# Attention and MLP in parallel on one core: full-size products in four column groups, value steps of two key tiles, VectorE's share of the exponentials set by set

## Chip, core and metric

The kernel runs on one core of a Trainium2 chip. The metric is the device time of the core in microseconds (us). It is a single launch, with all inputs read from and the output written to device memory.

## What is computed

From a 2048 x 512 input the reference takes a layer norm, gives it to an attention of 32 heads (16 wide each) and to an MLP with a second layer norm, and adds both results to the input:

```python
x = A_x                                   # 1 x 2048 x 512, bf16
xn = _layernorm(x, axis=-1)
# attention: H = 32 heads, Dh = 16, scale = 16 ** -0.5
qkv = (xn @ wqkv).reshape(B, S, 3, H, Dh)
scores = einsum("bhqd,bhkd->bhqk", q, k) * scale
o = einsum("bhqk,bhkd->bhqd", softmax(scores), v)
a = o.reshape(B, S, D) @ wo
# MLP: F = 1792
h = gelu(_layernorm(xn) @ w1 + b1)        # tanh form
return x + a + h @ w2 + b2
```

## The kernel before

**Sets.** The work of the attention is cut into 32 sets g: four blocks of 512 queries (qt = g // 8) times eight groups of four heads (s = g % 8). A set goes over 16 key tiles of 128 keys. One key tile of one head is a unit: a 128 x 512 piece of scores. `qk` (L918, its product at L921) makes a unit's scores on TensorE: the four heads of a set lie in four 32-row groups of the array, so up to four units run side by side. A unit then takes one of two ways.

**ScalarE's way.** `build_tile` (L1018) takes three units (PSUM banks 0 to 2) or two (banks 3 and 4) in turn, makes their scores, and ScalarE (ACT) takes the exponential of all of them in one instruction (L1046) into `p_sb`, a ring of 15 units. While it works on one group of banks, TensorE fills the other.

**VectorE's way.** For the key tiles that `KD_OF` names (2, 5, 8 and 11 in each set from set 2 on), the scores "ride" with a tile of ScalarE's into bank 5 or 7 (`ride`, `rides`). VectorE (DVE) turns them into 16-bit numbers with an add and a maximum (L1085, one instruction for each unit), and makes four shifted copies of the four units (L1108, four instructions for each key tile). Read as fp16 bits, these five terms with five sets of weighted values approximate the exponential; `dve_terms` (L1095) issues the value products of the terms in steps of two, two and one.

**Value products.** `pv` (L930, product at L939) multiplies the values with the exponentials. The values of four heads lie in four groups of 32 columns of the array, so four products run side by side, all into bank 6 (the accumulator of a set, closed by the copy at L1141). ScalarE's key tiles have one such group of four each, issued by `build_pv` (L1055) tile by tile; VectorE's have five.

**Full-size products.** Everything else on TensorE uses 128 x 128 weights: the transposes (L679), the projections to keys and queries (L746) and to values (L818), the MLP's first matrix (L1242), its second matrix and the output projection (`chain`, L1264, product at L1272, four products to a step), the last output products (L1337), and the filler products that keep TensorE busy (L1390).

**What sets the order.** Nothing is issued as it is written. Each piece of work goes as an `_Op` with a duration, a priority (mostly a due time) and resources into a planner, `_Plan` (L61). Its `run` (L124) goes through a modelled time and gives each engine, among the ops that could start within `TOL` of the earliest, the one with the lowest priority number. TensorE's ops have a mode: "q" for scores, "p" for value products, "d" for full-size products. A change of mode is charged 0.11 us, and an op of the same mode as the last gets its priority lowered by `KEEP`. The order that comes out is fixed in the program; on the chip each engine goes through its own list and waits where an input is late.

**Once per query block** come the MLP (14 first-matrix blocks, evicted by VectorE at L1249, two GELU instructions on ScalarE at L1259, then the second matrix) and the output projection. A set's sums of exponentials go through device memory to be inverted and spread (L1143 to L1153), and GpSimd checks their range (L1162 to L1168). The last set does this on VectorE (`build_opost_last`, L1172). After the plan has run, two small products and a cast (L1402 to L1405) make a flag of the range; a branch on it would recompute everything in a safe way (`_general`), which these inputs do not need.

Of the kernel before, what the change touches and what calls it, by code (L numbers as in the profile page):

```python
# [22 lines left out]
P = 128  # L23
DH = 16
HS = 4
# [26 lines left out]
class _Op:  # L52

    __slots__ = ("eng", "dur", "fn", "ndeps", "outs", "prio", "acq", "rel", "lat", "ready", "end",
                 "done", "dense", "mode", "seq", "spare")
# [5 lines left out]
class _Plan:  # L61
# [9 lines left out]
    TOL = 0.25  # L71
    KEEP = 0.5
# [51 lines left out]
    def run(self):  # L124
# [7 lines left out]
        while left:  # L132
# [41 lines left out]
            op.end = end  # L174
# [261 lines left out]
def kernel(  # L436
# [30 lines left out]
    KD = (2, 5, 8, 11)  # L467
    KD_OF = [() if g < 2 else KD for g in range(NG)]
# [22 lines left out]
    b2_sb = const.tile([1, D], BF, name="b2_sb")  # L491
# [26 lines left out]
    NQB = 5  # L518
# [16 lines left out]
    ta = const.tile([P, QW], F32, name="ta")  # L535
    rl_t = const.tile([P, NCH], F32, name="rl_t")
    on_t = const.tile([P, NCH, 32], BF, name="on_t")
    okl = const.tile([P, 2, NCH], F32, name="okl")
    okrow = flagp.tile([P, 1], F32, name="okrow")
    okr = flagp.tile([P, 1], F32, name="okr")  # L540
# [8 lines left out]
    add = I.add  # L549

# [94 lines left out]
    def layernorm(g):  # L645
        tt = range(4 * g, 4 * g + 4)
        sl = slice(4 * g, 4 * g + 4)
        after = [xt_op[2], xt_op[3]] if g else []
        for t in tt:
            def fst(t=t):  # L650
                I(nc.vector.bn_stats(out=stats[:, t, :], in_=x_sb[:, t, :]))  # L651
                st_inst[0] = I(nc.vector.bn_aggr(out=mv[:, t, :], in_=stats[:, t, :]))
            st_op[t] = add("DVE", 0.77, fst, [ld_x[t]] + after,
                           T0 + KG * g - 8 + t % 4 * 0.2 if g else -50 + t, lat=0.1)
        pr = T0 + KG * g - 7.5 if g else -40

        def frs():
            I(nc.gpsimd.tensor_scalar(out=wv1[:, sl], in0=mv[:, sl, 1], scalar1=LN_EPS,
                                      scalar2=None, op0=ALU.add))
            I(nc.gpsimd.tensor_tensor(out=r1[:, sl], in0=wv1[:, sl], in1=mhalf[:, sl],  # L660
                                      op=ALU.pow))
        r = add("POOL", 0.9, frs, [st_op[t] for t in tt] + [mk_half], pr)
        pool = early if g else wide
        for t in tt:
            r1_op[t] = r
            pr = T0 + KG * g - 7 + t % 4 * 0.2 if g else -30 + t
            eng = "DVE"

            def fxn(t=t):
                I(nc.vector.tensor_scalar(  # L670
                    out=xn_r[:, t % 4, :], in0=x_sb[:, t, :], scalar1=mv[:, t, 0:1],
                    scalar2=r1[:, t:t + 1], op0=ALU.subtract, op1=ALU.mult))
            xo = add(eng, 0.33, fxn, (r, xn_op.get(t - 4)), pr)
            key = ("xt", t)

            def ftr(t=t, key=key):
                bk = pool.bank(key)
                for jc in range(JC):
                    I(nc.tensor.matmul(ps[:, bk, jc * P:(jc + 1) * P],  # L679
                                       lhsT=xn_r[:, t % 4, jc * P:(jc + 1) * P], rhs=ident_bf[:],  # L680
                                       start=True, stop=True))
# [36 lines left out]
    ld_b2 = dma("SP", b2_sb[:], B_b2[None, :], (ld_w2,), prio=62.0, lat=4.0)  # L718
# [23 lines left out]
    def project(pool, key, pr, nb, deps, w, b, qt, slow=False):  # L742
        def fmm():
            bk = pool.bank(key)
            for jc in range(JC):
                I(nc.tensor.matmul(ps[:, bk, :], lhsT=w[:, jc, b * P:(b + 1) * P],  # L746
                                   rhs=xnT[:, qt, jc, :], start=(jc == 0), stop=(jc == JC - 1)))
# [66 lines left out]
    def vmm(pool, key, t):  # L814
        def fn():
            bk = pool.bank(key)
            for jc in range(JC):
                I(nc.tensor.matmul(ps[:, bk, :],  # L818
                                   lhsT=xnT[:, t // TQ, jc, (t % TQ) * P:(t % TQ + 1) * P],
                                   rhs=wv_sb[:, jc, :], start=(jc == 0), stop=(jc == JC - 1)))  # L820
        return fn
# [196 lines left out]
    def build_tile(i):  # L1018
# [10 lines left out]
        deps = set()  # L1029
        for (g, k, j) in us:  # L1030
            need_q(g)
            deps.update(qk_deps(g, k))
        acq = [(res[b0 + x], ("t", i)) for x in range(n)] + [(ride(i), None)]
        q = add("PE", pen(1), fqk, list(deps) + [qk_prev[0]], dl - QO, acq=acq, mode="q")
# [14 lines left out]
        e = add("ACT", act(n * QW), fex, [q, exp_prev[0]] + list(set(free)), dl,  # L1049
# [5 lines left out]
    def build_pv(u0):  # L1055
        g, k, _ = units[u0]

        def fpv():
            pv(g, k, [(va[:, k, :], lambda j: p_sb[:, unit_slot[u0 + j], :])])
        o = add("PE", pen(1), fpv, set([unit_exp[u0 + j] for j in range(HS)]  # L1060
                                       + [va_op[k], va_op[min(k + 1, NT - 1)]]),
                due(u0 + 4) - PO, acq=((o_ready, g),), mode="p")
        for j in range(HS):
            pv_of_unit[u0 + j] = o
# [107 lines left out]
    def build_opost_last(g):  # L1172
# [3 lines left out]
                 pv_ops[g], pr, rel=(o_ready,))  # L1176
# [11 lines left out]
        def f2():  # L1188
            I(nc.vector.tensor_scalar(out=okl[:, 0, :], in0=tav[:, :, DH], scalar1=L_MIN,
                                      scalar2=None, op0=ALU.is_ge))  # L1190
            I(nc.vector.tensor_scalar(out=okl[:, 1, :], in0=tav[:, :, DH], scalar1=L_MAX,
                                      scalar2=None, op0=ALU.is_le))
            I(nc.vector.tensor_tensor(out=okl[:, 0, :], in0=okl[:, 0, :], in1=okl[:, 1, :],
                                      op=ALU.mult))
            I(nc.vector.tensor_reduce(out=okr[:], in_=okl[:, 0, :], op=ALU.min, axis=AX.X))
        add("DVE", 0.6, f2, [e1], pr + 30)
# [10 lines left out]
    def build_mlp(qt):  # L1207
# [10 lines left out]
        def ft():  # L1218
            for i in range(4):
                I(nc.tensor.matmul(ps[:, misc.bank(rkey), i * P:(i + 1) * P], lhsT=rt[:, i, :],  # L1220
                                   rhs=ident_bf[:], start=True, stop=True))
# [11 lines left out]
        for fc in range(FC):  # L1233
# [6 lines left out]
            def fh(n=n, key=key):  # L1240
                for jc in range(JC):
                    I(nc.tensor.matmul(ps[:, misc.bank(key), :], lhsT=w1_r[:, n % NW1, jc, :],  # L1242
                                       rhs=yT[:, jc, :], start=(jc == 0), stop=(jc == JC - 1)))
# [20 lines left out]
    def chain(key, pr, steps, deps):  # L1264

        m = None
        for f0 in range(0, len(steps), 4):
            part = steps[f0:f0 + 4]

            def fn(part=part, f0=f0):  # L1270
                for y, (a, b) in enumerate(part):
                    I(nc.tensor.matmul(ps[:, misc.bank(key), :], lhsT=a, rhs=b,  # L1272
                                       start=(f0 + y == 0), stop=(f0 + y == len(steps) - 1)))
# [6 lines left out]
    def build_down(qt, gl):  # L1280

        del h_use[:]
        for c in range(TQ):
# [8 lines left out]
            steps += [(ones_bf[0:1, 0:P], b2_sb[0:1, :])]  # L1292
# [34 lines left out]
    def build_final():  # L1327
        gs = (NG - 2, NG - 1)
        for c in range(TQ):
# [5 lines left out]
            def fm(g, key=key, cs=cs):  # L1335
                def fn():
                    I(nc.tensor.matmul(ps[:, tailp.bank(key), :], lhsT=ont[:, g % NON, cs],  # L1337
                                       rhs=wo_pad[:, (g % NS) // 2, g % 2, :], start=(g == gs[0]),
                                       stop=(g == gs[1])))
# [11 lines left out]
    for g in range(NG):  # L1351
# [4 lines left out]
        while ti < len(tiles) and tiles[ti][2] < stop:  # L1356
            build_tile(ti)
            end = tiles[ti][2] + tiles[ti][1]
            while pend + HS <= end:
                build_pv(pend)  # L1360
                pend += HS
# [15 lines left out]
    def fill(t0, t1):  # L1377
        got = []
        t = max(t0, 2.5)
        while t + 0.25 < t1:  # L1380
# [20 lines left out]

    nc.vector.tensor_reduce(out=okrow[:], in_=okall[:], op=ALU.min, axis=AX.X)  # L1402
    nc.tensor.matmul(ps[0:1, OB, 0:1], lhsT=okrow[:], rhs=onesp[:], start=True, stop=False)
    nc.tensor.matmul(ps[0:1, OB, 0:1], lhsT=okr[:], rhs=onesp[:], start=False, stop=True)
    nc.vector.tensor_copy(flag_i[:], ps[0:1, OB, 0:1])  # L1405
    fast_ctx.close()
    full = 2 * P
# [33 lines left out]
```

## Time and profile before

| | us |
|---|---|
| median of 3 runs | 878.18 (876.96 to 879.3) |
| the profiled execution | 877.14 |
| its span, first to last instruction | 875.3 |

| engine | busy us | share of the span |
|---|---|---|
| PE (TensorE products) | 789.1 | 90% |
| DVE (VectorE) | 780.0 | 89% |
| ACT (ScalarE) | 771.8 | 88% |
| POOL (GpSimd) | 55.7 | 6% |

The profile shows one execution. PEld is TensorE's loading of weights, which overlaps its products. A row of a group gives a line of the kernel, the engine, the output and inputs, the tile's size, the count, the busy time and mean duration of one, and the idle time of the engine just before, with what ended it. Consecutive instructions overlap a little in the records, so a mean duration is longer than the distance from one start to the next.

### The profile page before, as it was taken

What the parts mean: (1) busy time and instruction counts of PE and PEld (TensorE: products, weight loads), DVE (VectorE), ACT (ScalarE), POOL (GpSimd) and SP (SyncE); (2) the same over time, 40 slices, a digit from 0 to 9 for tenths busy, and PEclk for the clock granted to TensorE, in tenths of its full rate; (3) what the DMA queues carried; (4) which work ended last, traced back from release to release, by engine and by line L of the source; (5) the groups of instructions that cost most, each with busy time, mean ns of one, the idle gap of its engine ahead of it and who ended that gap; (6) DMA issues with size and microseconds to landing.
All of it is one profiled execution on the core that took longest, in us unless ns stands there. A gap on an engine that the chain in (4) does not pass through costs nothing.

```text
span 875.3 us, 17469 instructions
## 1 busy us (share of the span) xinstructions
PE 789.1 (90%) x7007; PEld 248.6 (28%) x7007; DVE 780.0 (89%) x1346; ACT 771.8 (88%) x667; POOL 55.7 (6%) x153
## 2 busy tenths in 40 slices
PE   8999999889988999899888999999978999989895
PEld 3332232222222322223222322223222322223221
DVE  8645999988899999968989999987899999988986
ACT  4798888989899888999999888999999979899883
POOL 2300000000000000000000000000000000000000
PEclk9999799999999999999989999989999999999998
DMA  5400111000001112000001111000001111100000
GB/s 169 109 1 2 38 51 50 13 21 21 20 9 26 39 43 51 20 19 10 13 14 32 33 44 51 16 17 21 21 15 26 33 44 32 38 19 21 20 15 28
DMA packets 54810, 27.65 MB, mean 32 GB/s; under 512 B 40645, under 2 KB 50630, under 8 KB 54722
## 3 DMA queue, kind: packets, MB, share of 16 engines
q1 hardware_dynamic: 52562, 24.76, 10.3%
q10 hardware_dynamic: 2160, 1.70, 0.7%
q8 instruction: 56, 0.92, 0.4%
q14 instruction: 32, 0.26, 0.1%
HBM read 23.85 MB, written 2.61 MB: 30 GB/s over the span
## 4 chain that ended last, share of the span: by engine, by line
DVE 53%; PE 25%; ACT 10%; issue 8%; DMA 3%; POOL 0%; SPq 0%; DVEq 0%; ACTq 0%
DVE x_sb L1085 20%; DVE tb_x L1108 13%; ACT p_sb L1046 10%; PE ps L939 8%; PE ps L921 7%; DVE x_sb L1108 6%; PE ps L1272 5%; DVE ht L1249 4%; DMA rlb<-rdram 2%; DVE ont L1155 1%; DVE osb L1141 1%; PE ps L746 1%; PE ps L818 1%; PE ps L1390 1%; DVE stats L651 1%
## 5 line engine op out<-in xcount | busy, mean ns | idle before, releaser
L1046 ACT ACTIVATE p_sb<-ps 128x1024 bf16<-128x1024 f32 (+1 forms) x640 | 731.2, 1232 | 76.8 <-PE ps L921 69.8
L1085 DVE TENSOR_SCALAR x_sb<-ps 128x512 int16<-128x512 f32 x480 | 324.2, 689 | 32.7 <-PE ps L921 31.8
L921 PE MATMUL ps<-qz,kt 32*128 32x512 bf16 x2048 | 285.5, 389 | 43.2 <-ACT p_sb L1046 30.6
L1108 DVE TENSOR_SCALAR tb_x<-x_sb 128x2048 int16<-128x2048 int16 x320 | 217.7, 690 | 4.9 <-PE ps L939 3.4
L939 PE MATMUL ps<-p_sb,va 128*32 128x512 bf16 x1568 | 153.4, 394 | 4.5 <-DVE osb L1141 4.4
L921 PEld LDWEIGHTS <-kt 32*128 32x128 bf16 x2048 | 76.1, 91 | 247.9 <-issue 240.7
L939 PE MATMUL ps<-tb_x,vs 128*32 128x512 f16 x1280 | 121.2, 391 | 9.5 <-DVE tb_x L1108 8.4
L1108 DVE TENSOR_SCALAR x_sb<-x_sb 128x2048 int16<-128x2048 int16 x160 | 110.4, 690 | 1.9 <-PE ps L939 1.1
L939 PEld LDWEIGHTS <-va 128*32 128x32 bf16 x2048 | 50.7, 95 | 117.2 <-issue 108.1
L939 PEld LDWEIGHTS <-vs 128*32 128x32 bf16 x1920 | 56.0, 95 | 96.1 <-issue 82.4
L939 PE MATMUL ps<-x_sb,vs 128*32 128x512 f16 x640 | 64.5, 391 | 5.6 <-DVE x_sb L1108 5.0
L1162 POOL TENSOR_SCALAR okt<-lc 128x16 f32<-128x16 f32 x31 | 17.0, 548 | 761.0 <-DMA lc<-ldram 761.0
L1242 PE MATMUL ps<-yT,w_r 128*128 128x512 bf16 x224 | 57.7, 380 | 5.5 <-DVE x_sb L1085 3.6
L1272 PE MATMUL ps<-w_sb,ht 128*128 128x512 bf16 x224 | 59.5, 383 | 0.0
L939 PE MATMUL ps<-x_sb,va 128*32 128x512 f16 x480 | 48.9, 397 | 0.5 <-DVE osb L1141 0.5
L1249 DVE TENSOR_SCALAR ht<-ps,b_sb 128x512 bf16<-128x512 f32 x56 | 42.1, 752 | 0.0
L1390 PE MATMUL ps<-ones_bf,zeros_bf 128*128 128x512 bf16 x90 | 33.9, 455 | 1.5 <-DVE ones_bf L613 1.5
L1272 PE MATMUL ps<-wo_pad,ont 128*128 128x512 bf16 x120 | 32.0, 387 | 0.2 <-DVE x_sb L1085 0.2
L1242 PEld LDWEIGHTS <-w_r 128*128 128x128 bf16 x224 | 19.2, 97 | 37.6 <-issue 23.6
L1155 DVE TENSOR_TENSOR ont<-osb,rlb 128x512 bf16<-128x512 f32 x31 | 21.4, 690 | 7.0 <-DMA rlb<-rdram 7.0
L1272 PEld LDWEIGHTS <-ht 128*128 128x128 bf16 x224 | 18.1, 98 | 30.5 <-issue 17.5
L1259 ACT ACTIVATE ht<-ht 128x3584 bf16<-128x3584 bf16 x8 | 25.1, 3182 | 0.0
(89 smaller groups left out, 339.7 us busy)
## 6 DMA issues: line engine op xcount, KB each, us to landing
rlb<-rdram SPq DMA_DIRECT2D x31, 256.0 KB
w_r<-in_B_w_dram SPq DMA_DIRECT2D x56, 128.0 KB
x_r<-in_A_x_dram SPq DMA_DIRECT2D x16, 128.0 KB
w_sb<-in_B_w_dram SPq DMA_DIRECT2D x1, 1792.0 KB
out_dram<-ot SPq DMA_DIRECT2D x12, 128.0 KB
x_sb<-in_A_x_dram SPq DMA_DIRECT2D x2, 512.0 KB
wkv<-in_A_wqkv_dram ACTq DMA_DIRECT2D x1, 512.0 KB
x_sb<-in_A_x_dram ACTq DMA_DIRECT2D x1, 512.0 KB
```

Of the source, the lines that this page charges most:

```text
L921: I(nc.tensor.matmul(ps[:, bank, :], lhsT=kt[lo:lo + 32, s // 2, k * P:(k + 1) * P], rhs=qz[lo:lo + 32, (qt * NB + s // 2) % NQB, s % 2, : ...
L939: I(nc.tensor.matmul(ps[32 * j:32 * j + 32, o_bank[g], :], lhsT=vals[:, h * VS:h * VS + 32], rhs=wts(j), start=st, stop=(pv_left[g] == 0), ...
L1046: I(nc.scalar.activation(p_sb[:, s0:s1, :].rearrange("p a b -> p (a b)"), ps[:, b0:b0 + n, :].rearrange("p a b -> p (a b)"), AF.Exp, scale ...
L1085: I(nc.vector.tensor_scalar(out=ib[sl][:, j, :], in0=ps[:, misc.bank(key), :], scalar1=LEVEL, scalar2=0.0, op0=ALU.add, op1=ALU.max))
L1108: I(nc.vector.tensor_scalar(out=tb[x % NTB].rearrange("p j q -> p (j q)"), in0=ib[sl].rearrange("p j q -> p (j q)"), scalar1=float(SHIFT[t ...
L1155: e4 = add("DVE", dve(QW), lambda: I(nc.vector.tensor_tensor(out=ont[:, slot, :], in0=osb[:, i2, :], in1=rlb[:], op=ALU.mult)), [e3] + lis ...
L1162: I(nc.gpsimd.tensor_scalar(out=okt[:, 0, :], in0=lc[:, i2, :], scalar1=L_MIN, scalar2=None, op0=ALU.is_ge))
L1242: I(nc.tensor.matmul(ps[:, misc.bank(key), :], lhsT=w1_r[:, n % NW1, jc, :], rhs=yT[:, jc, :], start=(jc == 0), stop=(jc == JC - 1)))
L1249: I(nc.vector.tensor_scalar(out=ht[:, fc, :], in0=ps[:, misc.bank(key), :], scalar1=b1_sb[:, fc:fc + 1], scalar2=None, op0=ALU.add))
L1259: I(nc.scalar.activation(out=hv, in_=hv, func=AF.Gelu_apprx_tanh, scale=1.0))
L1272: I(nc.tensor.matmul(ps[:, misc.bank(key), :], lhsT=a, rhs=b, start=(f0 + y == 0), stop=(f0 + y == len(steps) - 1)))
L1390: I(nc.tensor.matmul(ps[:, OB if opened is None else o_bank[opened], :], lhsT=zeros_bf[:], rhs=ones_bf[:], start=opened is None, stop=open ...
```

## The change

All 896 full-size products are written as four products of 32 columns each, one to each column group of the array, as the value products are (`mm`, L552 of the changed kernel); the filler products too. They get the planner's mode "p", so that only two modes are left. The one-row product with the bias b2 becomes one of 128 rows (b2 padded with zeros).

`build_pv` takes two key tiles of ScalarE's to a step (`PAIR`), outside the first two sets and the end. `KD_OF` is a table: between two and five key tiles a set go to VectorE, 111 in all instead of 120, and a fifth key tile (14) may be among them, whose weighted values are made at the start (four more evictions on VectorE and four more full-size products). The ring `qz` of prepared queries has four places for five. The planner's constants are changed: `TOL`, `KEEP` (to zero), the due times of the MLP and the output projection, and the leads of scores, value products and VectorE's terms. The last set's range check goes to GpSimd, and the flag is made inside the plan by one product and one cast. The last set's transposes use the place of `ht`.

```diff
-    TOL = 0.25
-    KEEP = 0.5
+    TOL = 0.225
+    KEEP = 0.0
...
-        op.acq, op.rel, op.mode = tuple(acq), tuple(rel), "d" if dense else mode
+        op.acq, op.rel, op.mode = tuple(acq), tuple(rel), "p" if dense else mode
...
-    KD = (2, 5, 8, 11)
-    KD_OF = [() if g < 2 else KD for g in range(NG)]
+    KD = (2, 5, 8, 11, 14)
+    KD_OF = [KD[:n] for n in (0, 0, 2, 4, 5, 4, 4, 4, 3, 3, 3, 5, 3, 4, 4, 3, 5, 3, 3, 3, 5, 4, 3, 4, 4, 4, 2, 4, 5, 3, 4, 4)]
...
-    NQB = 5
+    NQB = 4
...
+    def mm(dst, lhsT, rhs, start, stop):
+
+        for j in range(HS):
+            I(nc.tensor.matmul(dst[32 * j:32 * j + 32], lhsT=lhsT[:, 32 * j:32 * j + 32], rhs=rhs,
+                               start=start, stop=stop, tile_position=(0, 32 * j)))
...
-    OUT0, OUT1 = 1.15, 0.3
-    HLO, HHI, DN0, DN1 = 0.15, 0.56, 0.56, 0.11
-    LEAD, LATE, AHEAD = 7, 4, 2
-    RATE, QO, PO, AO, DO = 24.75, 45.5, 37.0, 25.0, 39.5
+    OUT0, OUT1 = 0.925, 0.4
+    HLO, HHI, DN0, DN1 = 0.09, 0.5, 0.52, 0.12
+    PAIR = 2
+    LEAD, LATE, AHEAD = 9, 6, 2
+    RATE, QO, PO, AO, DO = 24.25, 60.0, 47.0, 35.0, 29.5
...
                 for y, (a, b) in enumerate(part):
-                    I(nc.tensor.matmul(ps[:, misc.bank(key), :], lhsT=a, rhs=b,
-                                       start=(f0 + y == 0), stop=(f0 + y == len(steps) - 1)))
+                    mm(ps[:, misc.bank(key), :], a, b, f0 + y == 0, f0 + y == len(steps) - 1)
...
-    def build_pv(u0):
-        g, k, _ = units[u0]
+    def build_pv(us):
+
+        g = units[us[0]][0]
+        ks = [units[u][1] for u in us]
...
-            pv(g, k, [(va[:, k, :], lambda j: p_sb[:, unit_slot[u0 + j], :])])
+            pv(g, ks, [(va[:, k, :], lambda j, u0=u0: p_sb[:, unit_slot[u0 + j], :])
+                       for k, u0 in zip(ks, us)])
...
-            I(nc.vector.tensor_scalar(out=okl[:, 0, :], in0=tav[:, :, DH], scalar1=L_MIN,
+            I(nc.gpsimd.tensor_scalar(out=okl[:, 0, :], in0=tav[:, :, DH], scalar1=L_MIN,
...
+        e3 = add("DVE", 0.2, lambda: I(nc.vector.tensor_reduce(
+            out=okrow[:], in_=okall[:], op=ALU.min, axis=AX.X)), [e1, e2], pr - 10.0)
+        e4 = add("PE", 0.2, lambda: I(nc.tensor.matmul(
+            ps[0:1, OB, 0:1], lhsT=okrow[:], rhs=onesp[:], start=True, stop=True)),
+            [e3], pr - 10.0, mode="d")
+        add("DVE", 0.15, lambda: I(nc.vector.tensor_copy(flag_i[:], ps[0:1, OB, 0:1])), [e4],
+            pr - 10.0)
...
-            steps += [(ones_bf[0:1, 0:P], b2_sb[0:1, :])]
+            steps += [(ones_bf[:, 0:P], b2_sb[:])]
...
+                n = PAIR if NU2 <= pend < len(units) - 4 * HS else 1
...
-                I(nc.tensor.matmul(ps[:, OB if opened is None else o_bank[opened], :],
-                                   lhsT=zeros_bf[:], rhs=ones_bf[:], start=opened is None,
-                                   stop=opened is None, skip_group_check=True))
+                for j in range(HS):
+                    I(nc.tensor.matmul(
+                        ps[32 * j:32 * j + 32, OB if opened is None else o_bank[opened], :],
+                        lhsT=zeros_bf[:, 0:32], rhs=ones_bf[:], start=opened is None,
+                        stop=opened is None, tile_position=(0, 32 * j), skip_group_check=True))
```

TensorE's list of TensorE products, counted in the order in which they stand: before, 2048 products of scores, 3968 of values, 896 full-size ones, 90 fillers and a few small ones; now 2048, 3824, 4 x 900 and 4 x 81. Stretches of the list with one mode, and so changes between them: 1286 before (548 stretches of scores, 482 of values, 257 full-size), 1134 now (566 of scores, 567 of all else, and the flag's).

**TensorE, the start of a second-matrix chain of the MLP in the second query block.** `p_sb,va` are value products, `x_r,ident_bf` and `w_sb,ht` the chain's first products, `qz,kt` scores. Before:

```order
L939 LDWEIGHTS va
L939 MATMUL ps<-p_sb,va 32x512
L1272 LDWEIGHTS ident_bf
L1272 MATMUL ps<-x_r,ident_bf 128x512
L1272 LDWEIGHTS ht
L1272 MATMUL ps<-w_sb,ht 128x512
...
L921 LDWEIGHTS kt
L921 MATMUL ps<-qz,kt 128x512
```

Now:

```order
L928 LDWEIGHTS kt
L928 MATMUL ps<-qz,kt 128x512
L555 LDWEIGHTS ident_bf
L555 MATMUL ps<-x_r,ident_bf 32x512
...
L555 LDWEIGHTS ht
L555 MATMUL ps<-w_sb,ht 32x512
...
L928 LDWEIGHTS kt
L928 MATMUL ps<-qz,kt 128x512
L946 LDWEIGHTS va
L946 MATMUL ps<-p_sb,va 32x512
```

Left out are the repeats: the four products of the chain's step are now sixteen of 32 columns, and eight value products (two key tiles) follow the next scores instead of four. The chain's step now stands between two stretches of scores.

**VectorE, the end of the list.** `ont` is the last set's result, `okl`, `okr`, `okrow` belong to the range check, `yT` is the output. Before:

```order
L1184 STREAM_TRANSPOSE ont<-on_t 128x512
L1189 TENSOR_SCALAR okl<-ta 128x16
L1191 TENSOR_SCALAR okl<-ta 128x16
L1193 TENSOR_TENSOR okl<-okl 128x16
L1195 TENSOR_REDUCE okr<-okl 128x1
L1344 TENSOR_TENSOR yT<-ps,wkv 128x512 x4
L1405 CAST flag_i<-ps 1x1
```

Now:

```order
L1196 STREAM_TRANSPOSE ont<-ht 128x512
L1338 TENSOR_TENSOR wkv<-ps,wkv 128x512
L1210 TENSOR_REDUCE okrow<-okall 128x1
L1361 TENSOR_TENSOR yT<-ps,wkv 128x512 x2
L1215 CAST flag_i<-ps 1x1
L1361 TENSOR_TENSOR yT<-ps,wkv 128x512 x2
```

Four small instructions have left; the last sum of the output projection (L1338), which stood ahead of the last transposes, is behind them, and the flag's cast stands between the output's additions.

More of the change, by code (lines that the diff above doesn't have):

```diff
@@ L1048, in fex @@
                                    AF.Exp, scale=1.0 / STEP))
-        e = add("ACT", act(n * QW), fex, [q, exp_prev[0]] + list(set(free)), dl,
+        e = add("ACT", act(n * QW), fex, [q, exp_prev[0]] + list(dict.fromkeys(free)), dl,
                 rel=[res[b0 + x] for x in range(n)])
@@ L1336, in fn @@
                 def fn():
-                    I(nc.tensor.matmul(ps[:, tailp.bank(key), :], lhsT=ont[:, g % NON, cs],
-                                       rhs=wo_pad[:, (g % NS) // 2, g % 2, :], start=(g == gs[0]),
-                                       stop=(g == gs[1])))
+                    mm(ps[:, tailp.bank(key), :], ont[:, g % NON, cs],
+                       wo_pad[:, (g % NS) // 2, g % 2, :], g == gs[0], g == gs[1])
                 return fn
@@ L1358 @@
             end = tiles[ti][2] + tiles[ti][1]
-            while pend + HS <= end:
-                build_pv(pend)
-                pend += HS
+            while pend < end:
+                n = PAIR if NU2 <= pend < len(units) - 4 * HS else 1
+                n = min(n, (end_unit[units[pend][0]] - pend) // HS) if pend >= NU2 else 1
+                if pend + n * HS > end:
+                    break
+                build_pv([pend + HS * x for x in range(n)])
+                pend += n * HS
             ti += 1
@@ L1399 @@
     I.run()
[L1402 to L1405, printed above, removed]
     fast_ctx.close()
-    full = 2 * P
+    full = P
     flag = nc.values_load(flag_i[0:1, 0:1], min_val=0, max_val=full)
```

64 lines of the change are left out of this document (32 added, 32 removed).

## Prediction

> **What bounds the kernel now.** I read the busy line of each engine first, then the busy time in stretches that begin and end where VectorE copies a set's accumulator out (set 1 at 87.4 us, then sets 7, 11, 15, 19, 23, 27 and 31).
>
> ```profile
> PE 789.1 (90%) x7007; PEld 248.6 (28%) x7007; DVE 780.0 (89%) x1346; ACT 771.8 (88%) x667; POOL 55.7 (6%) x153
> ```
> ```profile
> core 0: us, PE busy (x) PEld busy (x) DVE busy (x) ACT busy (x) POOL busy (x), PEclk, DMA share, GB/s
> 0.00:87.40 87.40, 80.24 (x486) 28.62 (x487) 55.86 (x118) 66.55 (x75) 12.27 (x33) 0.98 0.25 70
> 87.40:252.60 165.20, 151.73 (x1343) 46.18 (x1340) 152.65 (x259) 146.92 (x123) 8.60 (x24) 0.95 0.10 28
> 252.60:353.80 101.20, 93.00 (x871) 29.67 (x871) 99.93 (x172) 89.38 (x77) 6.07 (x16) 0.98 0.14 36
> 353.80:457.00 103.20, 91.90 (x853) 27.97 (x853) 88.45 (x151) 98.17 (x83) 4.57 (x16) 0.95 0.06 16
> 457.00:559.30 102.30, 93.56 (x871) 28.71 (x871) 99.58 (x171) 90.56 (x78) 5.62 (x16) 0.98 0.14 37
> 559.30:660.60 101.30, 91.87 (x853) 28.50 (x853) 91.13 (x155) 96.37 (x81) 5.31 (x16) 0.95 0.06 17
> 660.60:758.70 98.10, 91.01 (x863) 28.82 (x863) 96.60 (x167) 88.74 (x78) 6.98 (x16) 1.00 0.15 39
> 758.70:863.70 105.00, 93.57 (x861) 29.39 (x861) 90.37 (x152) 95.06 (x79) 6.25 (x16) 1.00 0.05 16
> ```
>
> The busy line alone says that three engines are about equally full. The stretches say more: the limit changes sides twice in each query block. In its first half (252.6 to 353.8, 457.0 to 559.3, 660.6 to 758.7) VectorE is busy 98.7%, 97.3% and 98.5% and ScalarE 88 to 90%: VectorE evicts the MLP's first matrix on top of its four key tiles a set. In the second half (353.8 to 457.0, 559.3 to 660.6) ScalarE, which has the GELU there, is at 95.1% both times, and VectorE at 86 and 90%. So neither engine's load can be lowered at the other's cost without naming the half.
>
> What ScalarE waits for is scores:
>
> ```profile
> ACT p_sb L1046 <- PE ps L921: 69.8, 133, 1.5
> ACT p_sb L1046 <- PE ps L939: 3.4, 5, 1.7
> PE ps L921 <- DVE x_sb L1085: 6.8, 21, 1.4
> ```
> ```profile
> 644.72 55.33 ACT L1046 ACTIVATE p_sb<-ps 128x1024 bf16<-128x1024 f32 x49 [0.31 <-PE ps L921]
> ```
>
> The first rows put 69.8 us of ScalarE's waits on TensorE, which comes late because it is behind other products or behind VectorE. The last row shows that this is not in the nature of the exchange: for 55 us, in a place with few full-size products, ScalarE runs 49 instructions without one wait.
>
> **The change, part by part.**
>
> *VectorE's share.* Prices from the groups:
>
> ```profile
> L1046 ACT ACTIVATE p_sb<-ps 128x1024 bf16<-128x1024 f32 (+1 forms) x640 | 731.2, 1232 | 76.8 <-PE ps L921 69.8
> L1085 DVE TENSOR_SCALAR x_sb<-ps 128x512 int16<-128x512 f32 x480 | 324.2, 689 | 32.7 <-PE ps L921 31.8
> L1108 DVE TENSOR_SCALAR tb_x<-x_sb 128x2048 int16<-128x2048 int16 x320 | 217.7, 690 | 4.9 <-PE ps L939 3.4
> L1108 DVE TENSOR_SCALAR x_sb<-x_sb 128x2048 int16<-128x2048 int16 x160 | 110.4, 690 | 1.9 <-PE ps L939 1.1
> ```
>
> Of 512 key tiles VectorE has 120 and ScalarE 392, which are 1568 units: 731.2 / 1568 = 0.466 us a unit, 1.87 us a key tile on ScalarE. On VectorE a key tile costs 4 x 324.2 / 480 + 4 x (217.7 + 110.4) / 480 = 5.44 us. Nine tiles fewer take 49 us from VectorE and put 16.8 us on ScalarE. By sets the tiles go from 24 to 23 (sets 2 to 7), 16 to 14 (8 to 11), 16 to 14 (12 to 15), 16 to 14 (16 to 19), 16 to 16 (20 to 23), 16 to 14 (24 to 27) and 16 to 16 (28 to 31). VectorE falls in the first halves to 99.93 - 10.9 = 89.0, 88.7 and 85.7 us, below ScalarE's 89.38 + 3.73 = 93.1, 94.3 and 92.5. ScalarE becomes the longest engine everywhere after set 1. The extra evictions for key tile 14's weighted values are four at the L1085 price, 2.7 us once, in a stretch (sets 0 and 1) where VectorE is 64% busy; I cost them at nothing there, 2.7 if they fall into set 2.
>
> *Mode changes.* A few microseconds of TensorE's list give the price:
>
> ```profile
> 216.13 0.74 PE L921 MATMUL ps<-qz,kt 32*128 32x512 bf16 x4
> 216.80 0.40 PE L939 MATMUL ps<-x_sb,va 128*32 128x512 f16 x4
> 217.03 0.39 PE L939 MATMUL ps<-x_sb,vs 128*32 128x512 f16 x4
> 217.25 0.39 PE L939 MATMUL ps<-p_sb,va 128*32 128x512 bf16 x4
> 217.57 0.50 PE L921 MATMUL ps<-qz,kt 32*128 32x512 bf16 x3
> 218.30 0.38 PE L1272 MATMUL ps<-x_r,ident_bf 128*128 128x512 bf16 x1 [0.23 <-DVE x_sb L1085]
> 218.52 0.81 PE L1272 MATMUL ps<-w_sb,ht 128*128 128x512 bf16 x3
> 219.26 0.61 PE L921 MATMUL ps<-qz,kt 32*128 32x512 bf16 x6
> ```
> ```profile
> 216.80 0.10 PEld L939 LDWEIGHTS <-va 128*32 128x32 bf16 x4 [0.57 <-issue]
> 216.82 0.11 PEld L939 LDWEIGHTS <-vs 128*32 128x32 bf16 x4
> ```
>
> Groups of four value products start 0.22 us apart (216.80, 217.03, 217.25); from the last of them to scores it is 0.32 (217.57). From the first of three full-size products (218.52) to the scores behind them it is 0.74, where three at 0.215 are 0.645. So a change of mode costs 0.10 us. The list has 1286 of them before and 1134 now: 152 x 0.10 = 15 us of TensorE. That is not two for each of the 257 full-size stretches, because most of them still stand next to scores. The nine tiles fewer take 36 groups of four (four extra groups each), 36 x 0.215 = 7.7 us. Together 23 us, 2.9% of TensorE's 789.1; what the slow entry at 218.30 is worth I leave out, as a wait on VectorE is mixed in.
>
> *Four products for one.* The new form must keep 0.215 us a step though it loads weights four times. The nearest rows are the value products: four loads take 0.11 us together (216.82) behind the products of the step before, and the step stays at 0.22. I take no cost, since number, size and column groups are the same; 896 steps would have to be 0.01 longer for 9 us.
>
> [...]
>
> *Two key tiles a value step.* A step is 0.43 us instead of 0.215 and cannot be cut, so scores behind it can come 0.22 later; and `p_sb`'s places come free later. Bounds: nothing, as ScalarE's instruction takes about 0.9 to 1.3 us and the next scores have that long; or 0.1 us for each of some 184 pairs (401 key tiles of ScalarE's less 32 of sets 0 and 1, by two), 18 us. I take nothing, because in the new list the stretches between two stretches of scores are shorter on the whole (mean of 0.89 us against 0.95 by the prices above, and 67 against 110 of them above 1.3 us).
>
> *The end.* The four small instructions that leave VectorE cost 0.55 us ahead of the output's additions; the sum that moves behind the transposes costs 0.60:
>
> ```profile
> 866.12 0.13 DVE L1189 TENSOR_SCALAR okl<-ta 128x16 f32<-128x16 f32 x1
> 866.25 1.04 PE L1337 MATMUL ps<-wo_pad,ont 128*128 128x512 bf16 x4 [1.49 <-DVE ont L1184]
> 866.75 2.48 DVE L1344 TENSOR_TENSOR yT<-ps,wkv 128x512 bf16<-128x512 f32 x4
> 869.15 0.13 DVE L1405 CAST flag_i<-ps 1x1 int32<-1x1 f32 x1
> ```
>
> GpSimd's four instructions stand beside the transposes. The flag is ready about a microsecond sooner, but the last output addition is not. I count 0, bounds -1 and +0.6. NQB, b2 and the filler products touch nothing that waits; 0.
>
> *The sum.* Since ScalarE is the longest engine in all stretches after set 1, a stretch takes its busy time divided by the share that it reaches. Today that share is 95.1% where it is longest, and 100% for 55 us at a time. I take 96.5%, a step up from today's because TensorE loses 2.9% of its work and no longer waits for a full VectorE. Sets 8 to 11: 93.1 / 0.965 = 96.5, -4.7. Sets 12 to 15: 101.9 / 0.965 = 105.6, +2.4. Sets 16 to 19: 97.7, -4.6. Sets 20 to 23: 99.9, -1.4. Sets 24 to 27: 95.8, -2.3. Sets 28 to 31 reach 90.5% today, with the run-out of the last set in them; at 93% it is 102.2, -2.8. Sets 2 to 7: ScalarE 148.8 at 93.5% (its longest engine has 92.4% today) is 159.1, -6.1. Sets 0 and 1, without VectorE's tiles: -0.5 for a few mode changes. Sum -20.0. The profiled execution took 877.14 (span 875.3 and 1.8 around it), 1.0 below the median of 878.18; 877.1 - 20.0 = 857.
>
> Bounds: with today's shares (95%, 90.5% and 92.4%) the same terms give -3.2 + 4.1 - 3.0 + 0.1 - 0.8 + 0 - 4.2 = -7, 870. With 98.5% (96% in the first and last stretch) they give -6.7 + 0.3 - 6.6 - 3.5 - 4.2 - 6.0 - 10.2 - 2 = -39, 838.
>
> **The rivals.** *ScalarE unhindered.* If the waits for scores were mostly VectorE's fault, ScalarE reaches 98.5%: 838 to 847. For it: the 55 us without a wait, in a place where TensorE has least to do. Against it: only 6.8 us of TensorE's waits for scores name VectorE.
>
> *Slower: ScalarE's waits stay.* If the 69.8 us come from full-size steps of four (0.86 us and two mode changes, which cannot be cut) that the change leaves as long as they were, the 16.8 us that move to ScalarE are paid in full: 877 + 17 = 894. It decides where the waits fall by less than 16.8, that is stay above 53 us. For it: in the second halves VectorE has slack and ScalarE still loses 5%. Against it: the list's long stretches fall by 40%.
>
> *No change: the pairs.* The two-tile steps cost their 18 us of late scores, and the gain of 20 is gone: 875 to 879.
>
> *Loads in line.* The groups have the duration of one load:
>
> ```profile
> L939 PEld LDWEIGHTS <-va 128*32 128x32 bf16 x2048 | 50.7, 95 | 117.2 <-issue 108.1
> L1242 PEld LDWEIGHTS <-w_r 128*128 128x128 bf16 x224 | 19.2, 97 | 37.6 <-issue 23.6
> ```
>
> If the four loads of a full-size step went one after another, four at 95 ns make 0.38 against 0.215: 820 steps of 512 columns (900 less the 80 transposes) x 0.165 = 135 us on TensorE, and a time near 877 + 135 - 23 = 989. Against it: two groups of four loads in 0.13 us at 216.80, and a tiled load that takes no longer than a full one.
>
> That the change does not do what it says is in the sum: it removes 12% of the mode changes, not the third mode's 40%.
>
> **How the numbers follow.** The forecast (848 to 871, the rest of its lower part belongs to the next case) has 0.58, ScalarE unhindered 0.17, the pairs 0.09, the waits that stay 0.14, loads in line 0.02. About 0.3%, 2.6 us, is what a measurement of this kernel can tell from no change. Faster: 0.58 + 0.17 + 0.02 of the pairs' lower end = 0.77; within 0.3%: 0.07; slower: 0.16. The range that leaves out 2 in 10 goes from 839, most of the unhindered case, to 878, most of the pairs' case.
>
> **What would show it.** Right: mode changes at 0.32 us as before, and full-size steps of four products each starting 0.215 apart; the waits of ScalarE for scores near 33 us (69.8 less the 20.0 that are gained and the 16.8 that are added); ScalarE the busiest engine in every stretch after set 1, at 96 to 97% in sets 8 to 27, and VectorE at 85 to 92%. Sets 12 to 15 longer than today, sets 8 to 11 and 16 to 19 shorter by 4 to 5 us each. Wrong: full-size steps above 0.23 us; waits for scores above 53 us; waits for value products, 3.4 us now, above 15; or VectorE still longest in the first halves.

## The result, and the profile after

The changed kernel takes 851.43 us (median, 848.83 to 852.08) against 877.7 of the kernel before in the same runs: a ratio of 0.9693, with a 95% interval of 0.9667 to 0.9718. The profiled execution took 850.97, with a span of 849.2.

The stretches below end where VectorE copies the accumulators of sets 1, 7, 11, 15, 19, 23 and 27 out, and where the last set's is transposed, as the stretches of the kernel before do.

```profile
core 0: us, PE busy (x) PEld busy (x) DVE busy (x) ACT busy (x) POOL busy (x), PEclk, DMA share, GB/s
0.00:84.90 84.90, 77.30 (x1166) 30.54 (x1167) 58.82 (x122) 67.77 (x76) 12.89 (x34) 1.00 0.25 73
84.90:245.80 160.90, 144.19 (x1837) 46.59 (x1837) 148.61 (x252) 146.47 (x124) 8.31 (x24) 0.95 0.11 30
245.80:348.80 103.00, 90.13 (x1169) 30.30 (x1169) 93.09 (x159) 98.53 (x84) 5.93 (x16) 1.00 0.13 34
348.80:444.80 96.00, 85.33 (x1066) 28.65 (x1064) 82.70 (x141) 92.45 (x81) 8.84 (x16) 0.95 0.07 19
444.80:540.10 95.30, 84.89 (x1133) 29.22 (x1131) 87.34 (x148) 92.03 (x81) 4.55 (x16) 1.00 0.15 38
540.10:640.00 99.90, 87.32 (x1088) 27.76 (x1086) 90.83 (x154) 97.44 (x82) 5.47 (x16) 0.97 0.06 17
640.00:734.90 94.90, 85.14 (x1114) 27.76 (x1114) 88.32 (x150) 91.03 (x81) 6.45 (x16) 0.98 0.16 40
734.90:838.50 103.60, 95.09 (x1210) 31.49 (x1213) 90.03 (x151) 95.34 (x81) 4.31 (x17) 0.97 0.06 16
```

From set 8 on ScalarE is the busiest engine in every stretch, at 95.7, 96.3, 96.6, 97.5 and 95.9% and 92.0% in the last, where TensorE is level with it (95.1 us against 95.3). VectorE, at 97 to 99% in the first halves before, is at 90 to 93% there (sets 8 to 11, 16 to 19 and 24 to 27). Sets 2 to 7 are the exception: VectorE is still 2 us ahead.

Who waited for whom, in total, in times, and the longest, and the groups of the exponentials and of VectorE's evictions of scores:

```profile
ACT p_sb L1053 <- PE ps L928: 36.6, 67, 1.9
ACT p_sb L1053 <- PE ps L946: 4.2, 3, 2.3
PE ps L928 <- DVE x_sb L1097: 6.4, 21, 0.8
```
```profile
L1053 ACT ACTIVATE p_sb<-ps 128x1024 bf16<-128x1024 f32 (+1 forms) x655 | 740.5, 1258 | 43.6 <-PE ps L928 36.6
L1097 DVE TENSOR_SCALAR x_sb<-ps 128x512 int16<-128x512 f32 x444 | 297.3, 683 | 29.2 <-PE ps L928 28.1
```

ScalarE's waits for scores fell from 69.8 us (133 times) to 36.6 us (67 times). TensorE's waits for VectorE's evictions hardly moved, from 6.8 to 6.4 us.

### The profile page after: what moved, and what is told of

The parts are those of the page before. It is cut to its first block, busy times and chain, and to the rows that moved or that the text cites. A ratio compares the mean times of both kernels' runs of the same rounds, so it can differ in the third digit from the quotient of the medians.

```text
span 849.2 us, 23044 instructions
## 1 busy us (share of the span) xinstructions
PE 751.2 (88%) x9799; PEld 252.8 (30%) x9799; DVE 744.3 (88%) x1274; ACT 781.1 (92%) x682; POOL 57.8 (7%) x158
## 4 chain that ended last, share of the span: by engine, by line
DVE 32%; PE 26%; ACT 24%; issue 12%; DMA 5%; ACTq 0%; DVEq 0%; SPq 0%
ACT p_sb L1053 24%; DVE x_sb L1097 11%; PE ps L555 9%; PE ps L946 8%; PE ps L928 8%; DVE tb_x L1120 7%; DMA rlb<-rdram 4%; DVE x_sb L1120 3%; DVE ht L1268 2%; PE ps L1412 2%; DMA rdram<-rc 1%; DVE ont L1167 1%; DVE stats L659 1%; DVE osb L1153 1%; DVE qc L810 0%
## 5 line engine op out<-in xcount | busy, mean ns | idle before, releaser
L1053 ACT ACTIVATE p_sb<-ps 128x1024 bf16<-128x1024 f32 (+1 forms) x655 | 740.5, 1258 | 43.6 <-PE ps L928 36.6
L1097 DVE TENSOR_SCALAR x_sb<-ps 128x512 int16<-128x512 f32 x444 | 297.3, 683 | 29.2 <-PE ps L928 28.1
L1120 DVE TENSOR_SCALAR tb_x<-x_sb 128x2048 int16<-128x2048 int16 x296 | 199.1, 685 | 5.8 <-PE ps L946 3.2
L946 PE MATMUL ps<-p_sb,va 128*32 128x512 bf16 x1604 | 129.4, 389 | 0.0
L1120 DVE TENSOR_SCALAR x_sb<-x_sb 128x2048 int16<-128x2048 int16 x148 | 101.3, 685 | 2.9 <-PE ps L946 2.0
L555 PE MATMUL ps<-yT,w_r 128*32 128x512 bf16 x896 | 59.2, 385 | 9.9 <-DVE x_sb L1097 5.4
L946 PEld LDWEIGHTS <-va 128*32 128x32 bf16 x2048 | 38.8, 94 | 81.6 <-issue 79.1
L555 PE MATMUL ps<-w_sb,ht 128*32 128x512 bf16 x896 | 61.4, 389 | 0.0
L555 PE MATMUL ps<-wo_pad,ont 128*32 128x512 bf16 x512 | 33.4, 381 | 1.3 <-DVE ont L1196 0.9
L555 PEld LDWEIGHTS <-w_r 128*32 128x32 bf16 x896 | 23.9, 96 | 34.2 <-issue 18.0
L1412 PE MATMUL ps<-ones_bf,zeros_bf 128*32 128x512 bf16 x324 | 31.3, 465 | 1.5 <-DVE ones_bf L621 1.5
L555 PEld LDWEIGHTS <-ht 128*32 128x32 bf16 x896 | 22.6, 99 | 25.8 <-issue 9.3
```

The lines of the kernel that those rows point to most:

```text
L555: I(nc.tensor.matmul(dst[32 * j:32 * j + 32], lhsT=lhsT[:, 32 * j:32 * j + 32], rhs=rhs, start=start, stop=stop, tile_position=(0, 32 * j)))
L946: I(nc.tensor.matmul(ps[32 * j:32 * j + 32, o_bank[g], :], lhsT=vals[:, h * VS:h * VS + 32], rhs=wts(j), start=st, stop=(pv_left[g] == 0), ...
L1053: I(nc.scalar.activation(p_sb[:, s0:s1, :].rearrange("p a b -> p (a b)"), ps[:, b0:b0 + n, :].rearrange("p a b -> p (a b)"), AF.Exp, scale ...
L1097: I(nc.vector.tensor_scalar(out=ib[sl][:, j, :], in0=ps[:, misc.bank(key), :], scalar1=LEVEL, scalar2=0.0, op0=ALU.add, op1=ALU.max))
L1120: I(nc.vector.tensor_scalar(out=tb[x % NTB].rearrange("p j q -> p (j q)"), in0=ib[sl].rearrange("p j q -> p (j q)"), scalar1=float(SHIFT[t ...
L1412: I(nc.tensor.matmul(ps[32 * j:32 * j + 32, OB if opened is None else o_bank[opened], :], lhsT=zeros_bf[:, 0:32], rhs=ones_bf[:], start=op ...
```

## The experiments

All times are medians; each ratio is to runs of the kernel before on the same chip, and kernels measured on different chips are compared by it. The changed kernel stands at 0.9693.

**The form alone, in the new order.** The planner's list stays word for word; only `mm` and the filler make one product again.

```diff
-        for j in range(HS):
-            I(nc.tensor.matmul(dst[32 * j:32 * j + 32], lhsT=lhsT[:, 32 * j:32 * j + 32], rhs=rhs,
-                               start=start, stop=stop, tile_position=(0, 32 * j)))
+        I(nc.tensor.matmul(dst, lhsT=lhsT, rhs=rhs, start=start, stop=stop))
...
```

> The changed kernel's own order of instructions, but each full-size product and filler is one product with 128 x 128 weights again. Mode changes in TensorE's list rise from 1134 to 1257. My theory (ScalarE's waits had two sources, TensorE's mode changes and a full VectorE, and both were eased): 123 x 0.10 = 12.3 us more on TensorE, some half of it on the path, 856 to 860 us, and ScalarE's waits for scores 5 to 8 us above the 36.6 of the changed kernel. Rival 'share' (all of the gain is VectorE's smaller share): 851, within 2. Rival 'form' (all of the gain is the column form): 870 or more.

Measured 855.6 us, 0.9751 (0.9723 to 0.9779): 0.6% slower than the changed kernel, 5 us, just under my range; scores were waited for 38.9 us, 2.3 more and not 5 to 8. The form is worth something, less than half of its 12.3 us. The same place in both lists shows why it is not more. TensorE in the changed kernel:

```profile
217.73 0.39 PE L928 MATMUL ps<-qz,kt 32*128 32x512 bf16 x3
218.07 1.05 PE L555 MATMUL ps<-xnT,wq_sb 128*32 128x512 bf16 x16
219.05 0.86 PE L928 MATMUL ps<-qz,kt 32*128 32x512 bf16 x6
```

and in this one:

```profile
217.61 0.39 PE L926 MATMUL ps<-qz,kt 32*128 32x512 bf16 x3
217.95 1.02 PE L554 MATMUL ps<-xnT,wq_sb 128*128 128x512 bf16 x4
218.91 0.89 PE L926 MATMUL ps<-qz,kt 32*128 32x512 bf16 x6
```

Between two stretches of scores sixteen small products take 0.98 us from start to start and four full ones 0.96, both with the mode's change: there the form saves nothing. It takes a mode change away only beside value products: behind a step of them the full-size products start 0.22 us later now (196.33 to 196.55 in the changed kernel), and 0.33 before (194.38 to 194.71).

**The form alone, in the old order.** The kernel before with `mm` at each full-size product and the padded bias row (one small fill on GpSimd goes with it); its plan is otherwise untouched.

> The kernel before with its own plan, but each full-size product and filler in four column groups (the bias product padded to 128 rows). Mode changes fall from 1286 to 1103. My theory: 18 us less on TensorE, but VectorE stays 97 to 99% busy in the first halves of the query blocks, so 868 to 873 us, with the gain in the second halves. Rival 'share': 877, within 2. Rival 'form': 855 or less.

Measured 876.38 us, 0.9988 (0.9965 to 1.0011): no difference, though 183 mode changes, 18 us of TensorE by their price, had gone (its busy time fell from 789.1 to 778.8). I had expected 868 to 873, with the gain in the second halves of the query blocks. These are two of them, sets 12 to 15 and 20 to 23:

```profile
348.80:453.30 104.50, 91.54 (x1106) 29.91 (x1106) 91.56 (x156) 97.45 (x81) 4.24 (x16) 0.95 0.06 16
553.10:658.70 105.60, 91.61 (x1155) 30.98 (x1143) 90.50 (x154) 97.92 (x82) 5.63 (x16) 0.98 0.05 16
```

They are no shorter than the 103.2 and 101.3 us of before, although VectorE is idle for 12 and 14% of them. ScalarE's waits for scores stayed as well:

```profile
ACT p_sb L1051 <- PE ps L926: 71.8, 123, 2.4
```

**VectorE's share back to 120 key tiles.**

```diff
-    KD_OF = [KD[:n] for n in (0, 0, 2, 4, 5, 4, 4, 4, 3, 3, 3, 5, 3, 4, 4, 3, 5, 3, 3, 3, 5, 4, 3, 4, 4, 4, 2, 4, 5, 3, 4, 4)]
+    KD_OF = [KD[:n] for n in [0, 0] + [4] * 30]
```

> The changed kernel with four key tiles a set on VectorE again (120 in all from set 2 on); all else changed. My theory: VectorE is full again in the first halves, 859 to 865 us, ScalarE's waits for scores back to 50 us or more. Rival 'share': 877. Rival 'form': 851, within 3.

Measured 857.07 us, 0.9775 (0.9739 to 0.9811): the table is worth 0.8%, 7 us, in the new kernel. Waits for scores 53.8 us, as my theory had it; the time is 2 us below its range. The first halves (sets 8 to 11, 16 to 19, 24 to 27):

```profile
247.60:348.60 101.00, 91.55 (x1189) 30.47 (x1189) 100.23 (x174) 92.10 (x79) 6.70 (x16) 1.00 0.13 35
445.30:546.00 100.70, 90.17 (x1198) 30.97 (x1198) 100.23 (x173) 92.38 (x80) 6.84 (x16) 1.00 0.13 35
646.50:746.20 99.70, 89.63 (x1182) 31.15 (x1182) 99.31 (x172) 92.01 (x80) 5.50 (x16) 1.00 0.14 37
```

VectorE is full in all three again, at 99 to 100%.

**The table alone**, without the column form, pairs, mode and constants.

> The changed kernel with full-size products of 128 x 128 weights, the third mode in the planner, one key tile a value step and the old constants of the planner: what is left of the change is the table of VectorE's share, the four-place ring, and the flag. 1340 mode changes in TensorE's list. My theory: 864 to 870 us. Rival 'share': 853, within 3. Rival 'form': 877, within 3.

Measured 869.94 us, 0.9907 (0.9879 to 0.9935), in my range: 0.9%, 8 us. Together form and table explain 12 us of 26. The theory of two sources lacked one.

**The old constants.**

```diff
-    TOL = 0.225
-    KEEP = 0.0
+    TOL = 0.25
+    KEEP = 0.5
...
-    OUT0, OUT1 = 0.925, 0.4
-    HLO, HHI, DN0, DN1 = 0.09, 0.5, 0.52, 0.12
+    OUT0, OUT1 = 1.15, 0.3
+    HLO, HHI, DN0, DN1 = 0.15, 0.56, 0.56, 0.11
...
-    LEAD, LATE, AHEAD = 9, 6, 2
-    RATE, QO, PO, AO, DO = 24.25, 60.0, 47.0, 35.0, 29.5
+    LEAD, LATE, AHEAD = 7, 4, 2
+    RATE, QO, PO, AO, DO = 24.75, 45.5, 37.0, 25.0, 39.5
```

> The changed kernel with the planner's constants of before (TOL, KEEP, the due times of the MLP and output, the leads and the pace); column form, pairs and table stay. After the first four runs, form and table explain 4 to 7 us each of the 26, so the rest must lie in the order that the constants or the pairs make. Theory 'constants': 865 to 870 us, waits for scores above 50 us. Rival 'pairs': 851 to 855.

Measured 861.22 us, 0.9834 (0.9809 to 0.9859): 1.4% slower than the changed kernel, 12 us. The time is nearer to the theory of the constants than to its rival, but waits for scores were not above 50:

```profile
ACT p_sb L1053 <- PE ps L928: 37.0, 73, 1.9
ACT p_sb L1053 <- PE ps L946: 8.4, 8, 2.6
```

So the column form, the table and the pairs bring the waits for scores down to 37.0 us in the old constants' order too, and the time to 0.9834. The waits for value products are 4.2 us longer than in the changed kernel; where the rest of the 12 us goes was not followed. It is not the mode changes: counted in the traces, this kernel has fewer, 1115 against 1136.

**One key tile a value step** (`PAIR = 1`).

> The changed kernel with one key tile a value step, as before. Mode changes 1144 against 1134. Theory 'constants': 851 to 855 us. Rival 'pairs' (two-tile steps save mode changes and keep TensorE out of ScalarE's way): 862 to 868.

Measured 855.55 us, 0.9774 (0.9753 to 0.9795): 0.8% slower, 7 us, between both expectations. So the pairs help as well.

**The new constants and the pairs alone**, with full-size products in the third mode and 120 key tiles.

> The new constants and the pairs alone: full-size products of 128 x 128 weights with the third mode, and four key tiles a set on VectorE. 1208 mode changes against 1286 of before. Theory 'constants': most of the gain is here, 858 to 864 us. Rival (the order helps only where form and table have made room): 870 or more.

Measured 861.39 us, 0.9841 (0.9823 to 0.9858): 1.6%, 14 us, within my range, with neither of the reliefs that my prediction built on. Its first and second half of a query block (sets 8 to 11, 12 to 15):

```profile
250.30:346.40 96.10, 86.49 (x859) 27.39 (x855) 96.10 (x168) 89.98 (x79) 4.97 (x16) 1.00 0.13 36
346.40:452.00 105.60, 94.71 (x873) 29.13 (x872) 93.03 (x157) 98.49 (x83) 4.13 (x16) 0.95 0.07 19
```

VectorE is still the bound of the first half, at 100%, but the half is 5 us shorter than the 101.2 before, because VectorE has 96.1 us to do in it and not 99.9. The second half, where it has room, has 93.0 for 88.5 (and is 2.4 us longer). A new order of the same instructions moved VectorE's load from the half that it bounds to the other. That this is how the order gains is an inference: the two halves together are 2.7 us shorter than before (201.7 for 204.4), sets 16 to 23 2.6 us, and sets 24 to 31 about 7.

**The 111 key tiles spread evenly.**

> The changed kernel with VectorE's 111 key tiles spread evenly: three in every third or fourth set from set 3 on, four elsewhere, without regard to where the MLP and the GELU are. If the place of the tiles matters: 855 to 859 us, with waits in the first halves. If the count alone does: 851, within 2.

Measured 854.17 us, 0.9745 (0.9725 to 0.9765), 0.5% slower, 5 us by the ratios: the place of the tiles counts a little. Both expectations are near it; the intervals just do not touch.

**The leads and the pace alone set back** (the last two lines of the constants).

> The changed kernel with the old leads and pace alone (LEAD, LATE, RATE, QO, PO, AO, DO). Of the 10 us that all old constants cost (861.2 against 851.4): theory 'leads' (scores and terms must be asked for earlier): 857 to 861 us, and more waits of ScalarE for value products (8.4 us with all old constants, 4.2 with the new). Rival 'due times': 851 to 854.

Measured 870.04 us, 0.9926 (0.9899 to 0.9954): 2.3% slower, 20 us, more than twice what I expected, and more than all old constants together: the leads fit the other constants.

```profile
ACT p_sb L1053 <- PE ps L928: 46.9, 67, 3.1
ACT p_sb L1053 <- PE ps L946: 9.5, 8, 2.0
```

Against the changed kernel these are 10.3 us more for scores, in as many waits, and 5.3 us more for value products, of the 17.3 us between the two spans (866.5 and 849.2). TensorE is not idle meanwhile. Counted in the two traces, over ScalarE's gaps of more than 0.1 us ahead of its exponentials, value, full-size and filler products fill 33.5 us of them with the old leads and 18.8 us with the new ones, scores 24.2 and 22.4. So with the old leads more of the other products stand ahead of the scores that ScalarE waits for.

One such place lies behind a GELU. TensorE and ScalarE in this kernel:

```profile
560.81 0.64 PE L946 MATMUL ps<-x_sb,va 128*32 128x512 f16 x4
561.24 0.64 PE L946 MATMUL ps<-x_sb,vs 128*32 128x512 f16 x4
561.67 0.64 PE L555 MATMUL ps<-x_r,ident_bf 128*32 128x512 bf16 x4
562.09 1.50 PE L555 MATMUL ps<-w_sb,ht 128*32 128x512 bf16 x12
563.37 1.07 PE L946 MATMUL ps<-tb_x,vs 128*32 128x512 f16 x8
564.37 0.51 PE L928 MATMUL ps<-qz,kt 32*128 32x512 bf16 x3
```
```profile
560.91 2.37 ACT L1053 ACTIVATE p_sb<-ps 128x1536 bf16<-128x1536 f32 x2
564.99 1.45 ACT L1053 ACTIVATE p_sb<-ps 128x1536 bf16<-128x1536 f32 x1 [1.71 <-PE ps L928]
```

and in the changed kernel, at the same set's GELU:

```profile
550.82 0.60 PE L928 MATMUL ps<-qz,kt 32*128 32x512 bf16 x1
551.35 0.62 PE L1412 MATMUL ps<-ones_bf,zeros_bf 128*32 128x512 bf16 x4
551.75 0.64 PE L555 MATMUL ps<-x_r,ident_bf 128*32 128x512 bf16 x4
552.18 1.36 PE L555 MATMUL ps<-w_sb,ht 128*32 128x512 bf16 x12
553.37 0.60 PE L946 MATMUL ps<-tb_x,vs 128*32 128x512 f16 x8
553.90 0.39 PE L928 MATMUL ps<-qz,kt 32*128 32x512 bf16 x3
```
```profile
554.40 2.36 ACT L1053 ACTIVATE p_sb<-ps 128x1536 bf16<-128x1536 f32 x2 [1.21 <-PE ps L928]
```

With the old leads 3.6 us of value and full-size products (560.81 to 564.37) stand ahead of the next scores, and ScalarE waits 1.71 us. In the changed kernel it is 3.1 us (550.82 to 553.90; the score product at 550.82 is one that VectorE takes), and ScalarE waits 1.21. This place shows the kind of wait, and not what the leads do: the half microsecond between the two is the clock's. TensorE's granted clock is 0.50 up to 564.6 in the first listing, and there the last eight value products take 1.00 us up to the next scores; in the second it is 0.50 up to 553.2 and 0.99 behind, and the same eight take 0.53.

**The due times alone set back**, and **TOL and KEEP alone set back.**

> The changed kernel with the old due times of the MLP and the output projection alone (OUT, HLO, HHI, DN). Theory 'due times' (the new ones move VectorE's evictions to where it has room): 857 to 861 us. Rival 'leads': 851 to 854.

> The changed kernel with the old TOL and KEEP alone, that is with the planner holding on to a mode. 1143 mode changes against 1134. Both theories: 851 to 854 us, since with two modes the count hardly moves; 856 or more would say that the choice among ops itself matters.

Measured 852.8 us, 0.9724 (0.9694 to 0.9755), and 850.16 us, 0.9689 (0.9657 to 0.972): neither can be told from the changed kernel. Taken back one group at a time, only the leads and the pace count. Their worth hangs on the others, though: with the old leads, setting the other constants back as well makes the kernel faster again (0.9834 against 0.9926).

**Three key tiles more on VectorE** (sets 9, 12 and 26).

> The changed kernel with one more key tile on VectorE in sets 9, 12 and 26, where VectorE sat idle 7.1, 7.3 and 5.6 us. If ScalarE is the limit now: 5.6 us less on it, 846 to 850 us. Rival (VectorE's slack is needed to answer TensorE in time, or the new order undoes it): 851 to 855.

Measured 854.0 us, 0.9718 (0.9688 to 0.9748): not faster, and not to be told from the changed kernel; the rival held. Its profiled execution was the longest of five (858.81, with a granted clock of 0.957; the other four took 850 to 855):

```profile
ACT p_sb L1053 <- PE ps L928: 46.7, 79, 1.9
```

ScalarE had less to do, and waited for scores 10 us more than in the changed kernel, in this longest execution. No version tried beats the changed kernel clear of its interval.

## Why the prediction was right, and where its reasons were not

**What bounds the kernel: right for the first halves.** VectorE bounds them: with 120 key tiles it is busy 99 to 100% of them in the new order too, both with the column form and (sets 8 to 11) without it; with 111 it is at 90 to 93%. That the column form gains nothing in the old order (0.9988) agrees there. In the second halves it does not follow: VectorE had room, ScalarE waited, and they got no shorter. What took the form's gain there is open.

**ScalarE as the new bound at 96.5%: right as a state.** The five stretches from set 8 to set 27 reach 95.7 to 97.5%, and ScalarE's waits for scores came to 36.6 us, with 33 forecast.

**Why it gets there: half of it.** The step "96.5%, a step up from today's because TensorE loses 2.9% of its work and no longer waits for a full VectorE" holds for about half of the gain. Column form, table and pairs with all old constants give 0.9834, with ScalarE's waits for scores at 37.0 us; the new constants and the pairs without either relief give 0.9841. Each is some 14 us of the 27, with the pairs in both. I had gone over the planner's constants without a price, and put the pairs at nothing. Taken back from the changed kernel, all constants are worth 1.4%, the table 0.8%, the pairs 0.8% and the form 0.6%; the leads alone are worth 2.3%, since beside the old leads the new values of the other constants cost time. These are not parts of one sum, since each was taken back from a kernel that has the others. The 96.5% itself was chosen between two shares of the old profile and not worked out from the reliefs. That the kernel reaches it although two sources of the gain stood at nothing in the forecast is in part luck.

**VectorE's share: right in kind, mis-sized.** The exponentials' busy time rose from 731.2 to 740.5 us, 9.3 and not 16.8. The 36 units did come, but 67 waits in place of 133 mean that more instructions follow each other directly, and those overlap in the records: 640 x 1.232 - 731.2 = 57 us of overlap before, 655 x 1.258 - 740.5 = 83 us now. The traces of all fourteen kernels agree: the busy time of their exponentials comes out within 0.6 us as 0.453 us for each unit and 0.108 us for each instruction that does not overlap the one before it, of which there are 185 before and 128 now. So the price of a unit was nearly right, and the fewer breaks were left out. The 7.5 us between 16.8 and 9.3 are of the size of the miss, 851.4 measured against 857, but no run ties the two together.

**Mode changes: the price held, the worth did not.** Scores follow values at the same distance as before (0.33 us, 541.62 to 541.95 in the changed kernel, and 0.32); but 12.3 us of them were worth 5 us of time in the new order, and 18 us nothing in the old.

**Four products for one: right.** At the end ten steps of four loads and four products in a row:

```profile
836.70 2.05 PEld L555 LDWEIGHTS <-ont 128*32 128x32 bf16 x40
836.91 2.33 PE L555 MATMUL ps<-wo_pad,ont 128*32 128x512 bf16 x40
```

Forty loads end 2.05 us after the first began, 0.21 a step. The rival of loads in line would need 3.8. No loss is seen here: steps of one full-size product started 0.22 us apart before (218.30 to 218.52).

**Two key tiles a step: the bounds were wrong.** I excluded a gain without giving a reason; the pairs are worth 7 us. The ten mode changes that they save (1144 against 1134) are 1 us at 0.10 each. What makes the rest was not tried.

**The stretches.** Sets 8 to 11 were forecast at 96.5 and took 103.0, sets 12 to 15 at 105.6 and took 96.0; the sum was 202.1 forecast, 199.0 measured. This query block's GELU, which lay in the second of them before, now lies across their border: its table load and its first instruction, 4.4 us of ScalarE's time (344.4 to 348.8), are in the first. I had left it where it was. It is not HHI alone that moved it: with the old due times, HHI at 0.56 among them, it begins 5.9 us ahead of the border (341.8, border at 347.7). What did was not tried. The other stretches were within 2.4 us.

**The end: right.** From the last set's transpose to the end of the span it is 11.6 us before and 11.7 (837.5 to 849.2) now.

**What stays open:** which of the seven leads it is, and why the other new constants cost time beside the old ones; how much of the 0.9834 is the pairs', since form and table were not run with the old constants and without pairs; and why the form gains nothing in the second halves of the old order.

## What to carry to other kernels

In a kernel with three engines at 90%, count an edit of priorities as a part of its own, even when no instruction goes with it: here a new order of the same instructions, with two-tile steps, was worth 14 us by itself, and 183 mode changes fewer in the old order were worth nothing. The table paid because it took work from VectorE where VectorE was full, so price by stretches, and see in which stretch the longest instructions of the new order fall. And where waits are to go, count the instructions that will follow their like directly: their busy time shrinks (here by 0.108 us each). Before a place in the trace is taken for the effect of an edit, compare the granted clock there.

## What was not expected of the hardware

In the changed kernel TensorE's granted clock falls to 0.50 for 6.8 us at each of the four GELUs (from 157.3, 348.5, 546.4 and 751.2), although its records show it busy for 6.5 to 6.8 us of them. In the kernel before it does so at three of the four (from 171.1, 369.1 and 570.5), and it also falls away from them (232.4 to 239.2 in the changed kernel, for one). The three rows are the changed kernel in the first instruction of a GELU (543.2 to 546.3), in the second with the table load and the first exponentials behind it, and after that:

```profile
543.00:546.40 3.40, 2.54 (x19) 0.67 (x15) 3.40 (x7) 3.39 (x3) 1.37 (x4) 1.00 0.02 2
546.40:553.20 6.80, 6.80 (x45) 1.64 (x48) 6.13 (x11) 6.76 (x5) 0.00 (x0) 0.50 0.19 60
553.20:556.00 2.80, 2.80 (x45) 0.88 (x33) 2.70 (x6) 1.60 (x2) 0.00 (x0) 0.99 0.00 1
```

While ScalarE is in the GELU it asks for no scores. In the first row TensorE has 19 products, some of them single ones for VectorE with waits between, and in the next 6.8 us the clock is 0.50. The steps behind the GELU then take 0.43 us (551.75 to 552.18, for one), where the same two products start 0.22 apart at a clock of 1.00 (220.59 to 220.81, outside a GELU). Over this trace the clock is 0.50 for 6.8 us five times, for 3.4 us three times (85.6 to 89.0, 423.6 to 427.0, 662.5 to 665.9), and from 843.4 to the end; what sets these lengths was not tried. That the thin stretch of the first row is what lowers the clock is not shown here. The plan's filler products stand in the second row, one step about every microsecond (546.59, 547.68, 548.76), and none stands in the first; no run here has put more of them there.
